# A static order of all steps of an attention and token-mixing kernel is replaced by another

## The chip, the cores and the metric

The kernel runs on one core of one Trainium2 chip. It is measured in device microseconds: three runs of the kernel as it was gave a median of 230.96 us (230.74 to 232.75).

## The reference

There are two parts, of 8 batches with 576 positions each. The first is attention with 8 heads of 64: one coarse attention on q, k and v averaged over groups of 4 positions, its result repeated 4 times, plus one local attention in which a position sees the positions less than 4 away.

```python
out_d = sm_attn(q_d, k_d, v_d)                 # 144 coarse positions
out_up = np.repeat(out_d, factor, axis=2)      # factor = 4
mask = np.abs(pos[:, None] - pos[None, :]) < factor
scores = np.where(mask, scale * np.matmul(q, k.transpose(0, 1, 3, 2)), -1e9)
...
return (out_up + out_local).astype(np.float32)
```

The second takes the result x, of 512 channels, through a rotation and two mixings.

```python
theta = x @ w_theta
zr, zi = x * np.cos(theta), x * np.sin(theta)
y = np.einsum('ts,bsd->btd', w_tok_r, zr) + np.einsum('ts,bsd->btd', w_tok_i, zi)
u = x + y
return (u + np.maximum(u @ w_ch, 0.0)).astype(np.float32)
```

## The kernel before, in words

All work is written as small steps, each with a two-letter name, a tuple of numbers (the batch first) and a place. The string ORDER lists the steps; a loop walks through it and issues each one. A chain of dependencies without semaphores (the function `pin`) keeps the instructions of each engine in the order in which they were issued. So ORDER sets the order on every engine, and with it which engine waits for whom. The letter behind a step is its engine (v VectorE, a ScalarE, g GpSimd); digits behind a TensorE step are its PSUM banks, of which there are 8; a digit or letter behind a load is its staging buffer, of which there are 14.

For one batch the steps are these. Loads are lk, lq (k and q, four each), lv and lw (two halves of a v tile, five each), all issued on SyncE's queue. Casts to bf16 are ck, cq and cv. TensorE transposes k and q in tp (for batch 7 a DMA does it, dk), and ev takes them out of PSUM into kT and qT. Means over 4 positions are kd and qd; pv and vd make those of v. The coarse attention is sd (scores), ed (exp), nd (numerator and denominator), xn (normalise), xd and xc (transpose into xdT). The local attention is ps (scores, three steps), ex (exp), mk (mask, a product with a 0/1 band), po (five steps), nm (normalise), xt (transpose) and xa (add both parts into xT). Steps ps, sd and po work on 64 rows of the array at a time.

The second part has th (x times w_theta), cs (cosine and sine on ScalarE), xm (x transposed back) and zz (the products z). The last 64 positions of a batch go another way: tt, ct, zt, zp, zc (dz, a DMA, for the later batches). Token mixing is mx, eight steps of nine matmuls, and ua adds x. Then come ch (u times w_ch), up and uc (u transposed; du, a DMA, for the later batches), rl (relu and add) and st (store). The last 64 positions of two batches are joined in ut, dt, ht, rt, ss and sr. Weights are loaded, cast and, for the token weights, transposed on TensorE in wp and taken out in wc, all before the first mx. The v of batch 0 takes a path of its own, by contiguous rows: loads l1, casts c1, transposes t1, evictions e1 (into xT of the other parity), then x1, which gathers the overlapping windows on TensorE, and cv.

Steps wm issue idle matmuls on a zero tile. Steps te and ts load ScalarE's tables for Exp and Sin ahead of their use. Buffers rotate by fixed rules: kT, z, uT and most others by the parity of the batch, pm through 4, tmp through 6, the denominators rl through 2.

In ORDER, a step's numbers are not written: each kind of step takes its next set of numbers, so that all steps of a kind run in one fixed sequence, by batch and then by number.

Of the kernel before, what the change touches and what calls it, by code (L numbers as in the profile page):

```python
# [57 lines left out]
l10 l11 c1g c1g k0 l12 lk3 l14 ckg c1v lk5 wm0b t101 c1g e1a kcg wm24 t123 e1a lq6 wm45 x12 cva ckg x13 cva x10 cvv  # L58
cqg lq7 lk8 lk9 tp45 cqg kcg kcg x12 lqa eva lqb kdg cvv kca cka wm62 tp67 lkc x13 lkd cvv eva ckv wm13 pv01 cqv lq0
la2 cqg lb1 tp45 qdv eva wm22 tp23 eva wm65 ps67 kdg vdv lq3 qdv ckg cka ps45 cag ex wm25 sd23 ex lb4 ed cbg lk5 sd01  # L60
cqg ps67 mkv ed po45 nm po23 nd45 nd01 la6 nm la7 xn xn lk8 mkg tp23 cag po45 ex xt6 po01 cqa eva la9 lqa mkg caa xd7
lqb ckg xca ckg nm tp23 nm xt4 xt5 lbd cag lbc cbg lb2 xt7 xa cqg lb1 eva lb0 cbg lb3 lb6 tp01 xa po23 th4 xa xm5 xa
lv7 cqg nm cbg th6 lw xt7 cbg th2 lv5 xm3 evv cbg ts cs tp01 lv8 lv9 cs cbg xa tt4 zz cs xm5 wp6 wp2 zz lw lw wp3 lw
lv4 lw cbg lqa zz ct lqd eva qdg ztv wp7 cba th4 wcv zp5 lkb xm6 wcv lkc kdg wcv wp2 wp3 wcv zcv wp0 wcv wp1 cs wp7
wca wcv ps45 lk2 lk1 wcv wcv ps23 te ex qdg ps01 lq0 zz kdv cva ex mx7 mx6 mx4 cvg ua sd23 cvg cvg mkv lc3 ex po01 ua
sd67 ed ed mkv mx5 ua nm po23 ua po01 cvg pv67 nm nm mkg vda mx4 ua po23 lq6 cqg po67 nd01 nm nd45 mx2 up3 xn lq7 ckg
xn cqg lk5 cka nm tp01 xd4 lk8 up5 uca eva xcv xt3 ucv lk9 tp67 cka xt4 xt0 ua ckg xt1 kdg lv4 xa xa xa mx5 xa eva lva
tp23 ua th4 xt0 lw xa evv cqg th5 xm1 lvb lcd lqc tt0 lw lk1 lv2 lv0 lw ts cs lw xm4 cqg cs tp67 ckg cqg th2 xm3 th5
ct lw cka zz tp01 cs qdg zz cs xm2 evv ztg lc6 lc5 zp4 mx6 ccg zz qdg zcv zz eva cvg mx7 ps45 te ex ua ps23 ua ckg kdv
ex mkv ps01 mx6 lq7 mx7 po45 sd23 ex lq8 lk3 kdg ed cvg sd01 cqg ckg ua lk4 lq9 mx6 tp23 mkv lva lw lvc lw nm ua tp45  # L70
up7 cvg mkv cvv ed mx0 eva cvg pv23 ccg ua ucv eva po67 po45 ua nm up1 nm vda ccg ccg ch0 nd67 lq1 xn nd23 lkb cqg cqa
tp45 uca qdg xn mx1 xd2 xt3 eva ps67 rl lq0 ua po45 xcv kdg qdg ps01 ch2 xa ckg ex mkg nm rl mx3 ps67 cqg lv2 cka po45
ex ua sd01 lkd xt2 ckg ex nm mx3 xt4 xt5 xa up2 ua cqa cqg tp67 cvv ed up3 xa evv uca th0 xa lv6 xt1 up2 xa lw th4 xm6
ucv ts cs uca th5 cvg lq5 ckg po01 cvg zz cs nm po23 xm7 cs ch6 nm tt4 tp01 lw ct tp23 th5 rl mkg ch4 lq7 zz st eva
evv rl po67 sd01 cs cqg cvg ztg po23 ch5 nm nm rl ch4 lv8 lw te ed cvg st pv67 vda zp0 zca lk4 cka lk3 lk1 tp23 cqa
mkg ckg lq9 lqb rl qdg lva lw xm1 eva ckg utg lv0 zz lw xm5 ch4 nd67 lvc zz xn lw nd01 mx5 lvd xn mx6 st ps23 rl lv2
ua po01 kdg nm ps45 ua mx7 lk5 ex xd0 cqa xt1 ex up6 ua xcv ucv lk6 kdv tp23 cqg utg mx0 tp45 qdg xa ua eva sd67 xt2
lv8 xt3 ch1 eva xa mkg ed xa th0 mkv rl cvg lk3 lw xt6 xt7 xa xa lw lk1 cvg th2 mx1 ua ts cs xm3 cvg tt0 zz th6 st lq4
cs cvg cka po45 dt cvg ckg ct po23 th7 mx1 ztg lk7 cs lvb nm pv45 cs ckg po67 cqg kdg lw nm ua sd23 mx0 cvg nm te ed
zp1 tp67 vdv zcv ht2 tp45 xm1 rt lw ua lq9 mx3 eva zz ps67 eva ua lva qdg po45 nm ex ps01 lq0 ex xm2 up3 zz lqc nd67  # L80
uca lvd tp45 cqa xm2 qdg xn nd01 zz mx3 cka cka xn mx2 xd0 up1 lk2 lv6 kdg st ua mx3 cqa mkv lw uca xcv eva tp67 xt0
up1 lk5 ua ua cva ucv xt4 xa mx5 st xa st eva ps23 mkg sd01 qdg po67 lw ed ua nm lv3 xt4 mx5 xt6 cva mx7 po01 ua ex
sd23 xa xa po45 lw nm cvg th6 nm lq4 cqv xt0 lw ed cvv xa ts cs tp23 mkv lv8 th1 cs xm4 ua ch5 kdg lw rl ch6 lv9 eva
tt0 th1 th7 xm5 pv23 utv ct ztg zz up0 ss cqg cs zz vdv mx1 uca ua xm0 lv1 lw st zz cs tp45 lv7 cvg lv0 cvg lqb nd23
xm7 ch1 eva kdg rl nd45 xn mx0 rl xn dz ch1 sr ps23 ps45 lw lw qdg lw te ex lka zz po67 ua mx0 ex ps23 cqa ex nm rl ua
lkd ps67 mkv po45 mx1 up0 mkg nm ckg sd23 po45 ua mkg lqc nm ex sd67 utg cka cvg lv6 uca mx1 ch0 cva xt4 ua st st xd1
xca cvg mx5 ed mx1 ed up2 lw xa ua rl xt3 ua uca pv45 cqg po67 xa lq4 nm po01 xt2 cvv th3 up6 vda ucv lq3 xt7 mx4 ch5
ckg st dk8 cqa xt6 nm xa rl st dkb th2 xa cqg nd01 ch5 ckg xm7 xa xn evg ht6 ts cs eva dt tt3 zz du nd01 lv5 rl du cs
ct xm5 qdv th7 cva xn zz cs mkg th2 cs dk2 ztg ua lv1 eva dk9 mx3 dz ua st xm7 kdg rt zz evg ch5 xm4 up2 uca qdg sr zz
xd3 lw mx6 xcv mx4 xt7 po01 ps23 te ex ua rl ua mx6 kdg nm po45 utv du xa ua po01 ps23 xt7 xa mx6 ex xt7 th2 nm ua xa  # L90
ts cs mkg lw ch3 du lv7 mx6 st nm sd45 rl cvg ps01 ua ss po23 nm te ex xt7 mx6 xt2 mx3 xa ed xa po01 lw du mkg ua st
# [666 lines left out]
```

## Time and profile before

| What | Value |
|---|---|
| median of 3 runs | 230.96 us (230.74 to 232.75) |
| span of the profiled execution | 229.4 us |
| mean granted TensorE clock | 0.996 |
| TensorE matmul busy | 219.7 us (96%) |
| VectorE busy | 185.6 us (81%) |
| ScalarE busy | 159.3 us (69%) |
| GpSimd busy | 144.1 us (63%) |
| TensorE on the chain that ended last | 86% of the span |
| moved by DMA | 49.35 MB, mean 215 GB/s |

The profile is of one execution, which is not one of the three runs; its own time is its span plus what lies around it, and the median of the runs is 1.56 us above the span. Matmuls are pipelined, so a busy TensorE is not one at its peak. A line such as L610 is a line of the kernel before. PE is TensorE, PEld its weight loads, DVE VectorE, ACT ScalarE, POOL GpSimd, SP SyncE and SPq its queue of DMA issues.

### The profile page before, as it was taken

The page shows a single profiled execution, that of the slowest core. Times are in us where ns is not written, and L with a number is a line of the kernel's source. Part 1 is how long each engine was busy: PE and PEld are TensorE (multiplying, and loading weights), DVE is VectorE, ACT ScalarE, POOL GpSimd, SP SyncE. Part 2 cuts the span into 40 slices and gives each one's busy share as a digit, 9 for nine tenths or more (in the row PEclk, how much of TensorE's full clock was granted, in tenths as well). Part 3 has the DMA queues.
Part 4 walks back from the last instruction along what each step waited for, and adds up shares of the span by engine and source line. Part 5 has one row for each costly group of instructions (what it writes and reads, how often), then busy time and mean ns, then how long its engine had stood idle before and what let it go on. Part 6 is the DMA issues. An engine that isn't in the chain of part 4 may idle for free.

```text
span 229.4 us, 8506 instructions
## 1 busy us (share of the span) xinstructions
PE 219.7 (96%) x3491; PEld 154.2 (67%) x3491; DVE 185.6 (81%) x377; ACT 159.3 (69%) x239; POOL 144.1 (63%) x190
## 2 busy tenths in 40 slices
PE   7898899999999999999999999899999999999992
PEld 2455778696778765776788667676676665677740
DVE  5168999999899899797898969979898889476382
ACT  2389899759987899689887896779879258600000
POOL 7768999929999989991984456892697310200000
PEclk9999999999999999999999999999999999999998
DMA  6999999999989999999998007996576357376677
GB/s 181 387 391 391 268 190 222 374 271 226 235 270 249 248 345 177 231 261 233 291 220 211 21 17 191 302 214 126 136 132 187 68 118 206 74 207 160 94 239 241
DMA packets 76647, 49.35 MB, mean 215 GB/s; under 512 B 61120, under 2 KB 61120, under 8 KB 76608
## 3 DMA queue, kind: packets, MB, share of 16 engines
q1 hardware_dynamic: 76608, 48.81, 83.4%
q8 instruction: 27, 0.44, 0.8%
q14 instruction: 12, 0.10, 0.1%
HBM read 33.98 MB, written 9.44 MB: 189 GB/s over the span
## 4 chain that ended last, share of the span: by engine, by line
PE 86%; DVE 7%; DMA 3%; issue 2%; SPq 1%; ACT 0%; POOL 0%; DVEq 0%
PE PS L610 30%; PE PS L548 12%; PE PS L635 12%; PE PS L304 5%; PE PS L531 4%; PE PS L512 3%; DMA st<-in_v_dram 3%; PE PS L587 2%; PE PS L483 2%; PE PS L448 2%; PE PS L560 2%; DVE tmp L521 2%; PE PS L624 2%; PE PS L652 2%; PE PS L453 1%
## 5 line engine op out<-in xcount | busy, mean ns | idle before, releaser
L610 PE MATMUL PS<-WT,z 128*128 128x288 bf16 x576 | 77.9, 286 | 0.2 <-issue 0.2
L610 PEld LDWEIGHTS <-z 128*128 128x128 bf16 x576 | 54.3, 98 | 15.8 <-issue 0.9
L615 DVE TENSOR_TENSOR uT<-PS,xT 128x288 bf16<-128x288 f32 x64 | 28.8, 452 | 11.8 <-PE PS L610 10.9
L548 PE MATMUL PS<-wth,xT 128*128 128x512 bf16 x128 | 32.2, 379 | 0.0
L635 PE MATMUL PS<-wch,uT 128*128 128x512 bf16 x128 | 31.1, 379 | 0.0
L569 POOL TENSOR_TENSOR zT<-xT,cst 128x512 bf16<-128x512 bf16 x7 | 8.1, 1153 | 34.0 <-ACT cst L566 34.0
L521 DVE TENSOR_TENSOR tmp<-PS,rl 128x512 bf16<-128x512 f32 x40 | 27.7, 692 | 1.4
L502 POOL TENSOR_TENSOR pm<-pm,band 128x1024 bf16<-128x1024 bf16 (+1 forms) x14 | 25.0, 1789 | 4.5 <-ACT pm L491 4.5
L537 DVE TENSOR_TENSOR xT<-PS,xdT 128x464 bf16<-128x464 f32 (+1 forms) x40 | 24.0, 629 | 3.0 <-ACT xdT L471 2.0
L640 DVE SCALAR_TENSOR_TENSOR osb<-PS,ur 128x512 f32<-128x512 f32 x32 | 21.8, 685 | 4.7 <-PE PS L635 4.2
L491 ACT ACTIVATE pm<-PS 128x1024 bf16<-128x1024 f32 (+1 forms) x24 | 20.4, 879 | 6.5 <-PE PS L483 6.5
L553 ACT ACTIVATE cs<-PS,pihc 128x512 bf16<-128x512 f32 x32 | 22.2, 693 | 1.6 <-PE PS L548 1.4
L720 ACT ACT_TABLE_LOAD x15 | 19.2, 1283 | 0.3
L331 POOL TENSOR_TENSOR two<-kT 128x580 f32<-128x580 bf16 x13 | 15.0, 1152 | 7.0 <-ACT kT L317 5.3
L635 PEld LDWEIGHTS <-uT 128*128 128x128 bf16 x128 | 11.9, 98 | 11.1
L554 ACT ACTIVATE cs<-PS 128x512 bf16<-128x512 f32 x32 | 19.2, 601 | 0.0
L594 DVE TENSOR_TENSOR z<-PS,cs 128x1024 bf16<-128x1024 bf16 x24 | 16.0, 682 | 2.3 <-PE PS L587 1.8
L548 PEld LDWEIGHTS <-xT 128*128 128x128 bf16 x128 | 11.3, 98 | 9.6 <-DVE xT L537 0.2
L331 POOL TENSOR_TENSOR two<-qT 128x576 f32<-128x576 bf16 x13 | 14.9, 1145 | 4.3 <-ACT qT L317 4.0
L438 ACT ACTIVATE pd<-PS 128x864 bf16<-128x864 f32 x16 | 13.8, 888 | 5.0 <-PE PS L427 4.9
L397 POOL CAST v_w<-st 128x512 bf16<-128x512 f32 x26 | 16.8, 672 | 0.0
L317 ACT COPY qT<-PS 128x1152 bf16<-128x1152 bf16 x13 | 14.6, 1121 | 2.0 <-PE PS L304 2.0
(116 smaller groups left out, 427.0 us busy)
## 6 DMA issues: line engine op xcount, KB each, us to landing
st<-in_k_dram SPq DMA_DIRECT2D x32, 288.0 KB, 6.0
st<-in_q_dram SPq DMA_DIRECT2D x32, 288.0 KB, 6.1
st<-in_v_dram SPq DMA_DIRECT2D x70, 128.0 KB, 5.2
out_dram<-osb SPq DMA_DIRECT2D x32, 256.0 KB, 2.4
st<-in_v_dram SPq DMA_DIRECT2D x4, 288.0 KB, 3.2
st<-in_moe_w_tok_r_dram SPq DMA_DIRECT2D x4, 288.0 KB, 6.5
st<-in_moe_w_tok_i_dram SPq DMA_DIRECT2D x4, 288.0 KB, 7.4
st<-in_moe_w_theta_dram SPq DMA_DIRECT2D x4, 256.0 KB, 6.3
```

What stands on the lines that cost most here:

```text
L331: nc.gpsimd.tensor_tensor(out=t, in0=src[:, :, 0:2], in1=src[:, :, 2:4], op=ALU.add)
L491: nc.scalar.activation(out=pm[(3 * b + u) % NPM][:, :, 0:n].rearrange("p e c j w -> p e (c j w)"), in_=at.pop(("ps", b, u))[:, :, 0:4 * W ...
L502: EW[w].tensor_tensor(out=t, in0=t, in1=m, op=ALU.mult)
L521: nc.vector.tensor_tensor(out=tmp[(NCH * b + c) % NTMP].rearrange("p g (j d) -> p g j d", d=D), in0=ps[:, :, :, 0:D], in1=r.unsqueeze(3).t ...
L537: nc.vector.tensor_tensor(out=xT[b % 2][:, :, CH * c:CH * c + cnt].rearrange("p e (m j) -> p e m j", j=4), in0=at.pop(("xt", b, c))[:, :, ...
L548: nc.tensor.matmul(out=ps, lhsT=xT[b % 2][:, dc, P * c:P * c + P], rhs=wth[:, dc, :], start=(dc == 0), stop=(dc == 3))
L553: nc.scalar.activation(out=t[:, 0, :], in_=ps, func=AF.Sin, bias=pihc, scale=1.0)
L554: nc.scalar.activation(out=t[:, 1, :], in_=ps, func=AF.Sin, bias=0.0, scale=1.0)
L610: nc.tensor.matmul(out=ps, lhsT=z[b % 2][:, j, P * dc:P * dc + P], rhs=WT[:, j, cols], start=(j == 0), stop=(j == 8))
L615: nc.vector.tensor_tensor(out=uT[b % 2][:, dc, cols], in0=at.pop(("mx", b, i)), in1=xT[b % 2][:, dc, cols], op=ALU.add)
L635: nc.tensor.matmul(out=ps, lhsT=uT[b % 2][:, dc, P * c:P * c + P], rhs=wch[:, dc, :], start=(dc == 0), stop=(dc == 3))
L640: nc.vector.scalar_tensor_tensor(out=o, in0=at.pop(("ch", b, c)), scalar=0.0, in1=ur[b % 2][:, c, :], op0=ALU.max, op1=ALU.add)
```

## The change

ORDER is another list. It holds the same steps, with new engines for some of them, new banks and staging buffers, and it writes out the numbers of every step (`tp010.01` is tp with batch 0, half 1, operand 0, in banks 0 and 1), so that steps of a kind can stand in any sequence: ps 2 ahead of ps 0, mx 5 ahead of mx 2. The list follows a planned time over all engines, with loads taken to land later than in the plan of the old list, and with idle matmuls placed where TensorE is half idle. There are 20 idle matmuls (37 before), all ahead of the first sd and behind it none, 13 table loads (15 before), and five buffers rl instead of two. Among the steps that may go to several engines VectorE gets two more ev, two more qd, three more zt, one more ck, cq, uc and xc, and one less kd, mk, vd and zc and three less wc.

```diff
 ORDER = """
-l10 l11 c1g c1g k0 l12 lk3 l14 ckg c1v lk5 wm0b t101 c1g e1a kcg wm24 t123 e1a lq6 wm45 x12 cva ckg x13 cva x10 cvv
-sd67 ed ed mkv mx5 ua nm po23 ua po01 cvg pv67 nm nm mkg vda mx4 ua po23 lq6 cqg po67 nd01 nm nd45 mx2 up3 xn lq7 ckg
...
+lk02.0 lk03.1 kc3.a l100.2 lq01.3 l101.4 lq00.5 l103.6 ck02.a l102.7 lk01.8 ck03.v lk00.9 kc0.g lq03.a c100.v kc2.g
+nd11.23 xn11.v ck20.g po10.01 lq33.d tp211.45 nm10.v ev211.a po11.67 lv23.1 nm11.v mx07.2 ua07.v xd1.3 lw21 xc1.v
...
-    rl = tiles(2, [P, 2, 4], "rl", FP32)
+    rl = tiles(NCH, [P, 2, 4], "rl", FP32)
...
-        r = rl[c % 2]
+        r = rl[c]
...
-    todo = {kind: iter(seq) for kind, (_, seq) in STEPS.items()}
+    todo = {(kind,) + tuple(args) for kind, (_, seq) in STEPS.items() for args in seq}
     for word in ORDER.split():
-        kind, place = word[:2], word[2:]
+        word, _, place = word.partition(".")
+        kind, args = word[:2], tuple(int(x) for x in word[2:])
...
-        STEPS[kind][0](*next(todo[kind]), place)
+        todo.remove((kind,) + args)
+        STEPS[kind][0](*args, place)
         pin()
```

Two places show what moves. The first is the start of SyncE's queue of loads, here as it was (st0 to st11 are the staging buffers, each takes one tile of two heads).

```order
L367 DMA st0_127<-in_v_dram 128x576
L367 DMA st1_128<-in_v_dram 128x576
L367 DMA st2_129<-in_v_dram 128x576
L288 DMA st3_130<-in_k_dram 128x576
L367 DMA st4_131<-in_v_dram 128x576
L288 DMA st5_132<-in_k_dram 128x576
L288 DMA st6_133<-in_q_dram 128x576
L288 DMA st7_134<-in_q_dram 128x576
L288 DMA st8_135<-in_k_dram 128x576
L288 DMA st9_136<-in_k_dram 128x576
L288 DMA st10_137<-in_q_dram 128x576
L288 DMA st11_138<-in_q_dram 128x576
```

And the same twelve places of SyncE's queue now (L399 loads v, L320 k and q).

```order
L320 DMA st0_130<-in_k_dram 128x576
L320 DMA st1_131<-in_k_dram 128x576
L399 DMA st2_132<-in_v_dram 128x576
L320 DMA st3_133<-in_q_dram 128x576
L399 DMA st4_134<-in_v_dram 128x576
L320 DMA st5_135<-in_q_dram 128x576
L399 DMA st6_136<-in_v_dram 128x576
L399 DMA st7_137<-in_v_dram 128x576
L320 DMA st8_138<-in_k_dram 128x576
L320 DMA st9_139<-in_k_dram 128x576
L320 DMA st10_140<-in_q_dram 128x576
L320 DMA st11_141<-in_q_dram 128x576
```

Both are the twelve tiles of batch 0. The loads of v have moved from the front to the middle, and two of k have come to the front.

The second place is VectorE behind its constants, up to the first mask product (pm). As it was (v_w0 is v by windows, k_tm and q_tm are k and q in bf16, qd0 the means of q, vd0 those of v):

```order
L395 CAST v_w0_70<-PS_61 128x8x64 x3
L297 CAST k_tm1_75<-st9_136 128x8x64
L297 CAST k_tm1_75<-st9_136 128x64
L297 CAST q_tm1_78<-st10_137 128x8x64
L297 CAST q_tm1_78<-st10_137 128x64
L323 TENSOR_REDUCE qd0_68<-qT0_64 128x288
L413 CAST vd0_72<-PS_61 128x8x64
L416 CAST vd0_72<-PS_61 32x4x64 x2
L323 TENSOR_REDUCE qd0_68<-qT0_64 128x288
L502 TENSOR_TENSOR pm0_83<-pm0_83,band_145 128x1024
```

And the stretch of VectorE now that begins with the cast of the tenth load and reaches the first mask product.

```order
L329 CAST k_tm0_74<-st9_139 128x8x64
L329 CAST k_tm0_74<-st9_139 128x64
L329 CAST q_tm1_78<-st10_140 128x8x64
L329 CAST q_tm1_78<-st10_140 128x64
L329 CAST q_tm1_78<-st11_141 128x8x64
L329 CAST q_tm1_78<-st11_141 128x64
L427 CAST v_w0_70<-PS_61 128x8x64
L355 TENSOR_REDUCE qd0_68<-qT0_64 128x288
L427 CAST v_w0_70<-PS_61 128x8x64
L355 TENSOR_REDUCE qd0_68<-qT0_64 128x288
L427 CAST v_w0_70<-PS_61 128x8x64
L534 TENSOR_TENSOR pm0_83<-pm0_83,band_148 128x1024
```

The casts of k and q now stand ahead of the evictions into v_w0, of which there are still three and which now alternate with the means; vd0 has gone to ScalarE. Ahead of this stretch VectorE casts one tile each of k, v and q and takes out one transposed q.

More of the change, by code (lines that the diff above doesn't have):

```diff
@@ L98 @@
+rl72.v st71 st72 ch70.2 rl70.v st70 ht3.0 rt3.v sr3 ch73.1 rl73.v st73 ss3
 """
@@ L722 @@
             continue
-        STEPS[kind][0](*next(todo[kind]), place)
+        todo.remove((kind,) + args)
+        STEPS[kind][0](*args, place)
         pin()
-    for kind in todo:
-        assert next(todo[kind], None) is None, kind
+    assert not todo, todo
     assert set(x[0] for x in at) <= {"v", "ot"}, at
```

109 lines of the change are left out of this document (70 added, 39 removed).

## The prediction

> **What bounds the kernel now.** I read the span and the shares of the engines first, then the engines by stretches, then the chain that ended last, then the waits.
>
> ```profile
> core 0: 229.4 us, clock 0.996
> ...
> PE 219.7 (96%) x3491; PEld 154.2 (67%) x3491; DVE 185.6 (81%) x377; ACT 159.3 (69%) x239; POOL 144.1 (63%) x190
> ...
> 0.00:30.00 30.00, 26.00 (x411) 15.85 (x412) 20.24 (x54) 19.91 (x26) 24.56 (x52) 1.00 0.97 323
> 30.00:90.00 60.00, 59.76 (x1146) 44.66 (x1144) 55.84 (x108) 52.32 (x82) 53.53 (x68) 1.00 1.02 255
> 90.00:140.00 50.00, 50.00 (x840) 36.97 (x839) 42.62 (x87) 42.28 (x63) 33.81 (x42) 1.00 0.79 184
> 140.00:150.00 10.00, 9.06 (x224) 6.49 (x223) 8.52 (x17) 5.86 (x10) 7.32 (x8) 1.00 1.04 285
> 150.00:220.00 70.00, 70.00 (x859) 48.14 (x857) 53.77 (x108) 38.90 (x61) 24.87 (x24) 1.00 0.66 140
> ```
>
> The stretches give the stretch, its length, then busy time of PE, PEld, DVE, ACT and POOL with instruction counts, the granted clock, the DMA share and GB/s. From 30 to 220 us PE is busy for 59.76 + 50.00 + 9.06 + 70.00 = 188.82 of 190 us, at full clock. So 1.2 us of idle time is all that a better order can take out of these 190 us without removing PE work, and the change removes none of it there: the same transposes and matmuls run. What is not PE-bound is the head, up to the first token-mixing matmul (mx, L610), and the tail.
>
> ```profile
> 2.67 5.95 DMA st<-in_v_dram
> ...
> 9.39 0.69 PE PS L378 x9
> ...
> 14.59 0.69 DVE v_w L395
> 15.28 0.91 DVE k_tm L297 x2
> 16.19 0.94 DVE q_tm L297 x2
> 17.13 1.26 DVE qd L323
> 18.39 0.60 DVE vd L413
> ...
> 19.78 1.35 DVE qd L323
> ...
> 22.83 0.52 issue
> ...
> 28.83 0.99 PE PS L548 x4
> ...
> 38.36 3.41 PE PS L610 x27
> ```
>
> This is the chain of work in order of time (start, length, what). In the head it runs through v of batch 0 (its landing, then its transpose on PE) to the eviction into v_w on VectorE, where the last casts of k and q (15.28, 16.19) stand behind the v_w evictions although they have nothing to do with them. VectorE then carries most of the chain until the normalised tiles are transposed. The first channel matmul (th, L548) starts at 28.83, mx at 38.36.
>
> **The change part by part.**
>
> The first 12 loads (SP). They are the same 12 tiles, of one size, in another order.
>
> ```profile
> 4.73 1.74 SPq L288 DMA_DIRECT2D st<-in_k_dram  x2
> 6.51 1.72 SPq L288 DMA_DIRECT2D st<-in_q_dram  x2
> ...
> st<-in_k_dram SPq DMA_DIRECT2D x32, 288.0 KB, 6.0
> ```
>
> The 10th load is issued near 6.4 and the 12th near 8.2 (near the ends of these rows); with 6.0 us to landing (the median of such a load) they are there by about 12.4 and 14.2, whichever tiles they are. In the new order the 10th is k 0,0 and the last two are q. VectorE now casts k 0,0 (ck00), q 0,3 and q 0,2 one behind another. At 0.93 us each (rows 0.91 and 0.94), from 12.4, the third ends at 15.2; in the row above it ends at 17.13. VectorE is 1.9 us ahead there.
>
> VectorE up to the first mx. Behind that point the new order gives VectorE more before the last input of mx (zc0): three v_w evictions, one mask multiply, the copy xc0 and the mean qd10; and less: vd0, zt0 and three copies of WT.
>
> ```profile
> L502 DVE TENSOR_TENSOR pm<-pm,band 128x1024 bf16<-128x1024 bf16 x7 | 5.7, 814 | 0.0
> ...
> L323 DVE TENSOR_REDUCE qd<-qT 128x288 bf16<-128x1152 bf16 x3 | 4.0, 1346 | 0.0
> ...
> L279 DVE COPY WT<-PS 128x576 bf16<-128x576 bf16 x8 | 3.1, 442 | 0.0
> ...
> L471 DVE COPY xdT<-PS 128x576 bf16<-128x576 bf16 x5 | 2.2, 447 | 0.0
> ...
> L395 DVE CAST v_w<-PS 128x512 bf16<-128x512 f32 x3 | 2.1, 692 | 6.3 <-PE PS L390 6.3
> ...
> L569 DVE TENSOR_TENSOR zT<-xT,cst 128x512 bf16<-128x512 bf16 x1 | 0.7, 724 | 0.0
> ```
>
> Added: 3 x 0.69 + 0.81 + 0.45 + 1.35 = 4.7. Removed: vd0 (18.39 to 19.78 in the chain, 1.4) + 0.72 + 3 x 0.44 = 3.4. So 1.3 us of the 1.9 is given back, and I take **-0.6** for the head. All five normalisations and both batch means (nm, xn) now stand ahead of the first xa, so th begins no earlier than before, with more of the small PE steps already done. Bounds: -2.4 if none is given back and the half microsecond of "issue" at 22.83 goes too; above nothing, +1.7, worked out at the clock rival below.
>
> Idle matmuls. The order has 20 where it had 37, all in the head.
>
> ```profile
> L715 PE MATMUL PS<-warm 128*128 128x512 bf16 x37 | 10.2, 407 | 0.0
> ...
> L227 PE MATMUL PS<-warm 128*128 128x512 bf16 x6 | 2.7, 630 | 1.3 <-DVE warm L198 1.3
> ```
>
> They fill time in which PE waits, so taking 17 away is worth nothing; what it costs if their cover is gone is the clock. The first six took 630 ns each as a mean, 2.7/6 = 0.45 us of PE apiece, the later ones 10.2/37 = 0.28: PE starts at a lower speed. The granted clock reads 1.00 as a mean of every stretch above, so after those first six nothing was slow. In the new order only three idle matmuls follow the first six before the first k transposes, whose casts cannot be ready before about 6.3 (the second load's landing, then 0.9 of cast on VectorE behind its constants), and PE stands for about 1 us there; a slow start that lasts longer is a rival below. The Trainium skill ("TensorE: Matmul & The Clock Gate", Part 1) says that the array runs at half rate until it was busy through a free-running window of about 3.4 us, and falls back after an idle one. The slow first six agree with the first half of that; no run so far shows the fall.
>
> Switches of array shape. Steps ps, sd and po use 64-row tiles.
>
> ```profile
> 44.43 1.21 PE PS L610 x9
> ...
> 60.98 0.80 PE PS L483 x80
> ...
> 67.15 1.10 PE PS L610 x9
> ...
> 96.24 0.39 PE PS L483 x32
> ```
>
> An mx ahead of a po (44.43) occupies PE 1.21 us, one ahead of a transpose (67.15) 1.10, so going in costs 0.11. Three ps in a row (two of 32 matmuls, one of 16: two and a half units) take 0.80, one of 32 alone 0.39; so 1.5 units are 0.41, a unit 0.27, and coming out costs 0.12. Counted in the two orders from the first mx on, there were 22 ways in and 26 out (the others pass through pv, whose 6 ways in cost the same), and now 28 and 31 (with 5): 10 more, since lone steps stand between po steps (po10 tp211 po11, where po11 and po12 stood together). 10 x 0.11 = **+1.1**, on PE itself, with nothing to hide it.
>
> Waits that go and come.
>
> ```profile
> DVE uT L615 <- PE PS L610: 10.9, 21, 0.9
> ...
> PE PS L512 <- DVE tmp L521: 0.9, 1, 0.9
> ```
>
> Behind the head, PE's longest wait is that of po for a PSUM bank that nm must empty, once, 0.9 us. With another order this place does not exist in its old form; I count all of the 1.2 us as gone: **-1.2**. New ones of this kind come, since banks are as few as before (8) and the new order evicts each almost as soon as it is full, so that the next user follows closely. The trace cannot show them. Below: nothing. Above: the 3.4 us of the VectorE rival. I take **+1.0**, near to what the old order has, since it shares out the same banks in the same way.
>
> Off the path: one Exp table and one Sin table less on ACT (two loads, and ACT is at 42.28 of 50 us or under from 90 on); rl in five buffers instead of two, which only lets the normalisations run in any order; loads issued earlier against their casts, where PE waits for no landing behind the head.
>
> The tail.
>
> ```profile
> 202.80 14.33 PE PS L610 x117
> 217.14 6.91 PE PS L635 x32
> 224.04 0.88 PE PS L652 x4
> ```
>
> It was 13 mx, eight ch and ht3, with one VectorE step and two stores behind. Now it is again a run of mx and eight ch, with ht3 ahead of the last ch, one VectorE step and two stores: **0**. du73, the transposing DMA for the last results, has four ch (4 x 0.86) to cover it.
>
> Sum: 229.4 - 0.6 + 1.1 - 1.2 + 1.0 = 229.7 us of span. The median of the runs, 230.96, is 1.6 above this span, which lies around it. So **231.3 us**.
>
> **The rivals.**
>
> VectorE becomes the bound (slower). Between 30 and 90 us it is busy for 55.84 of 60, idle 4.2. Counted in the order from the first mx to the last step of batch 1, the new one gives it some 3.4 us more there: one more q or k eviction or mean (1.35), vd2 (1.4), two zt (2 x 0.72), one mask multiply less (0.81). 0.8 us stays idle. It decides once VectorE needs more waiting than that for its inputs; the 21 waits for mx in the row above, up to 0.9 each, say that it needs some. If it needs all 4.2, PE slips 3.4 in place of the 1.0: 229.7 + 2.4 + 1.6 = 233.7. Against: the VectorE steps that PE needs at once are few, and rl and ua of finished batches could lag. Place: th, po and mx waiting for xa, nm, zz or a bank of theirs between 45 and 95 us.
>
> Half clock in the head (slower). If full rate comes one window later, the nine idle matmuls ahead of the first v transposes last 9 x 0.45 = 4.1 in place of 9 x 0.28 = 2.5, and two transposes (0.69 at 9.39 in the chain) take twice as long, 1.2 more; less half a microsecond in which PE would wait for its casts anyway, some 2.3 us later for everything behind: the head is +1.7 in place of -0.6, and the time 233.6. For it: the head holds 17 idle matmuls fewer. Against: the granted clock stays at 1.00 with 4 us of gaps in the head now (PE 26.00 of 30).
>
> The head keeps its lead (faster). -2.4 in place of -0.6, and no new waits: 229.4 - 2.4 + 1.1 - 1.2 = 226.9, with 1.6 around it 228.5. For it: the casts of k and q no longer stand behind v. Against: the VectorE sum above.
>
> **How the numbers follow.** What counts as no change is within 1%, 228.65 to 233.27. The forecast, and what lies close to it, has 0.46; the head's lead 0.26; VectorE 0.19; the clock 0.09. The forecast's own range is 229.3 to 233.3, with new waits from nothing to 3 us. With the two slower rivals at 233.6 to 233.7, which may fall together with a wait of the forecast's kind, and the faster one with 1 us of doubt on its head, the range goes from 227.3 to 235.3. Faster than 1%: 0.26 (all of the head's lead). Slower: 0.28 (both of the others). Same: 0.46.
>
> **What would show it.** PE busy in the 10 us stretches from 40 to 220 within 0.3 of 10 each; the first mx between 36.5 and 38.5 in the chain; mx of 1.21 more often than before; VectorE busy for 58 or more of the 60 us from 30 to 90; a granted clock of 1.00 from the first stretch. I am wrong on the head if the first mx comes before 36 or after 39.5; wrong on the waits if PE loses over 3 us between 40 and 220; wrong on the clock if a stretch of the head shows less than 1.00 past 6 us.

## The result, and the profile after

The new order takes a median of 234.08 us (4 runs, 233.26 to 234.47) where the old one takes 230.96; the ratio is 1.0113, with a 95% interval from 1.0066 to 1.0160. Timed once more later, it took 235.32 us (6 runs, 233.43 to 236.09) beside 230.92 for the old order: 1.0176 (1.0136 to 1.0215). Ratios are of the means of the fast executions alone, while the medians are over all executions. The prediction was 231.3, within a range of 227.3 to 235.3, with "within 1%" as the likeliest case; the kernel came out slower, by 1 to 2 percent.

The profiled execution took 233.26 us, the fastest of the first four; its span is 231.6 us, so 1.7 us lie around it (1.6 was assumed). Its page says of the engines:

```profile
span 231.6 us, 8441 instructions
...
PE 219.9 (95%) x3474; PEld 154.5 (67%) x3474; DVE 185.6 (80%) x381; ACT 155.9 (67%) x242; POOL 139.2 (60%) x180
```

And by the same stretches as before, with the same columns (stretch, length, busy time of PE, PEld, DVE, ACT and POOL, granted clock, DMA share, GB/s):

```profile
0.00:30.00 30.00, 23.37 (x399) 15.09 (x400) 21.22 (x59) 21.11 (x28) 22.37 (x50) 1.00 0.95 333
30.00:90.00 60.00, 59.97 (x1126) 44.56 (x1125) 56.19 (x106) 53.23 (x85) 46.60 (x59) 1.00 0.89 263
90.00:140.00 50.00, 49.78 (x905) 36.31 (x902) 42.20 (x87) 41.37 (x63) 37.51 (x46) 1.00 0.75 193
140.00:150.00 10.00, 10.00 (x189) 7.15 (x188) 8.20 (x18) 8.49 (x16) 8.34 (x8) 1.00 0.58 148
150.00:220.00 70.00, 69.69 (x833) 48.30 (x831) 51.53 (x106) 31.72 (x54) 24.38 (x21) 1.00 0.69 140
```

PE is busy for 59.97 + 49.78 + 10.00 + 69.69 = 189.44 of the 190 us from 30 to 220. Before, it was 188.82. By this column PE stands still for less time than it did, and yet the span is 2.2 us longer. The column counts a matmul that waits a little, or takes a little longer because the array changes its shape, as busy.

So I took another measure: for each step of TensorE, the time from its start to the start of the next, less what a step of its kind takes when one of the same shape follows at once (1.10 us for mx, 0.86 for th and ch, 0.50 for tp, and so on; idle matmuls count for nothing). These shortest times sum to 196.80 us up to the last step, in both orders. What is left is lost:

| us | before | after | after, a second profile |
|---|---|---|---|
| lost up to the first mx | 19.05 | 19.55 | 20.17 |
| lost from there to the start of the last step | 8.03 | 9.76 | 11.51 |
| of that, switches of array shape | 5.25 (54) | 6.29 (64) | as many |
| of that, waits over 0.05 us | 1.81 (4) | 2.47 (19) | more, up to 1.2 each |
| from the start of the last step to the end | 5.52 | 5.45 | 5.46 |
| span | 229.4 | 231.6 | 233.9 |

Of the 2.2 us of the first profile, 0.5 lie in the head, 1.0 in switches and 0.7 in waits. The 0.5 is the difference of two single profiles and has scatter of its own: over the profiles that have one of the two heads unchanged, the first mx comes at 37.75 to 38.29 us in the old head (four) and at 38.55 to 39.38 in the new one (four), by the means 0.9 us later. The old order has four waits behind its first mx (1.13 us ahead of po54 at 146 us, 0.41, 0.16, 0.11); the new one has nineteen, the longest 0.37. The second profile (of the last run below; 235.65 us) is nearer to the median and has 2.3 us more of the head's and the waits' kind.

In the head of the new order, on PE (start, length, what; in brackets the idle time ahead of a group and what ended it):

```profile
3.79 1.49 PE L748 MATMUL PS<-warm 128*128 128x512 bf16 x3
6.90 1.14 PE L336 MATMUL PS<-ident,k_tm 128*128 128x128 bf16 x9 [1.62 <-ACT k_tm L329]
7.83 3.35 PE L748 MATMUL PS<-warm 128*128 128x512 bf16 x9
11.01 0.67 PE L410 MATMUL PS<-ident,z 128*128 128x128 bf16 x9
...
29.84 1.90 PE L580 MATMUL PS<-wth,xT 128*128 128x512 bf16 x8 [0.56 <-POOL uT L294]
...
38.80 1.40 PE L642 MATMUL PS<-WT,z 128*128 128x288 bf16 x10
```

Nine idle matmuls at 7.83 take 3.35 us, 0.37 each (the old order's later ones took 0.28), and the nine transposes at 6.90 take 1.14 where those at 11.01 take 0.67. TensorE runs at half speed here: where the clock came before these nine, in a run below, they took 2.11 us, 0.23 each. The trace's record of the granted clock begins, with 1.00, at 10.33 us (5.51 us in the profile of before); ahead of the first record the column of the stretches reads 1.00 too, so that it could not show this. The first th (L580) starts at 29.84, the first mx (L642) at 38.80.

On VectorE, in the same head:

```profile
13.93 0.96 DVE L329 CAST q_tm<-st 128x512 bf16<-128x512 f32 x4
15.51 0.69 DVE L427 CAST v_w<-PS 128x512 bf16<-128x512 f32 x1 [0.61 <-PE PS L422]
...
19.83 2.03 DVE L534 TENSOR_TENSOR pm<-pm,band 128x1024 bf16<-128x1024 bf16 x2
...
25.14 0.19 DVE L490 RECIPROCAL rd<-PS 72x8 f32<-72x8 f32 x1
...
28.60 2.28 DVE L569 TENSOR_TENSOR xT<-PS,xdT 128x464 bf16<-128x464 f32 x4 [0.51 <-PE PS L563]
```

In the old order the same first addition into xT stood at 27.55:

```profile
27.55 2.27 DVE L537 TENSOR_TENSOR xT<-PS,xdT 128x464 bf16<-128x464 f32 x4
```

The third cast ends at 13.93 + 0.96 = 14.89 (17.13 before), so VectorE was 2.2 us ahead. Then, but for two waits for PE (0.61 and 0.51), it works without a stop, and the first addition into xT comes 1.05 us later than before.

Last, two mx behind the first one, on PE. From its start to the start of the next step, an mx ahead of a step on 64 rows takes 1.21 us (64.45 to 65.66) and one ahead of a transpose 1.12 (66.04 to 67.16):

```profile
64.45 1.28 PE L642 MATMUL PS<-WT,z 128*128 128x288 bf16 x9
65.66 0.32 PE L515 MATMUL PS<-qT,kT 64*64 64x64 bf16 x16
...
66.04 1.28 PE L642 MATMUL PS<-WT,z 128*128 128x288 bf16 x9
67.16 0.67 PE L336 MATMUL PS<-ident,k_tm 128*128 128x128 bf16 x9
```

### The profile page after: what moved, and what is told of

It reads as the page before. It is cut to its first block, busy times and chain, and to the rows that moved or that the text cites. A ratio compares the mean times of both kernels' runs of the same rounds, so it can differ in the third digit from the quotient of the medians.

```text
span 231.6 us, 8441 instructions
## 1 busy us (share of the span) xinstructions
PE 219.9 (95%) x3474; PEld 154.5 (67%) x3474; DVE 185.6 (80%) x381; ACT 155.9 (67%) x242; POOL 139.2 (60%) x180
## 4 chain that ended last, share of the span: by engine, by line
PE 73%; DVE 4%; POOL 1%; issue 1%; DVEq 0%
PE PS L642 27%; PE PS L667 11%; PE PS L580 10%; PE PS L336 4%; PE PS L563 3%; PE PS L515 2%; PE PS L544 2%; PE PS L619 2%; PE PS L656 2%; PE PS L684 2%; PE PS L480 1%; PE PS L592 1%; PE PS L459 1%; PE PS L485 1%; DVE osb L672 1%; PE PS L437 1%
## 5 line engine op out<-in xcount | busy, mean ns | idle before, releaser
L642 PE MATMUL PS<-WT,z 128*128 128x288 bf16 x576 | 78.0, 286 | 0.0
L642 PEld LDWEIGHTS <-z 128*128 128x128 bf16 x576 | 54.2, 98 | 15.0 <-issue 0.3
L580 PE MATMUL PS<-wth,xT 128*128 128x512 bf16 x128 | 31.9, 379 | 0.6 <-POOL uT L294 0.6
L534 POOL TENSOR_TENSOR pm<-pm,band 128x1024 bf16<-128x1024 bf16 (+1 forms) x15 | 26.2, 1750 | 8.5 <-ACT pm L523 8.5
L363 POOL TENSOR_TENSOR two<-kT 128x580 f32<-128x580 bf16 x14 | 16.6, 1182 | 10.2 <-ACT kT L349 7.8
L580 PEld LDWEIGHTS <-xT 128*128 128x128 bf16 x128 | 11.6, 98 | 11.1 <-DVE xT L569 0.7
L349 ACT COPY kT<-PS 128x1152 bf16<-128x1152 bf16 x12 | 13.4, 1123 | 6.1 <-PE PS L336 4.5
L601 POOL TENSOR_TENSOR zT<-xT,cst 128x512 bf16<-128x512 bf16 x4 | 5.6, 1396 | 19.7 <-ACT cst L598 19.6
L662 POOL COPY ut<-uT 128x256 bf16<-128x256 bf16 x4 | 1.6, 397 | 26.1 <-DVE uT L647 26.1
L429 POOL CAST v_w<-st 128x512 bf16<-128x512 f32 x24 | 15.7, 678 | 0.0
```

The costliest lines, as they stand in the source:

```text
L534: EW[w].tensor_tensor(out=t, in0=t, in1=m, op=ALU.mult)
L580: nc.tensor.matmul(out=ps, lhsT=xT[b % 2][:, dc, P * c:P * c + P], rhs=wth[:, dc, :], start=(dc == 0), stop=(dc == 3))
L642: nc.tensor.matmul(out=ps, lhsT=z[b % 2][:, j, P * dc:P * dc + P], rhs=WT[:, j, cols], start=(j == 0), stop=(j == 8))
```

## The experiments

The theory going in was that the head costs 0.5 us, the switches 1.0 and small waits 0.7. The rivals were VectorE as the bound from 30 to 90 us, the late clock as the cause of it all, and the head alone.

**The clock released earlier** (new order, four more idle matmuls in the first group).

```diff
-wm.23 tp010.01 ev010.a
+wm.27 tp010.01 ev010.a
```

> The new order with seven idle matmuls in place of three in the first group behind the warm-up (L748), nothing else. They fill the gap from 5.3 to 6.9 us in which TensorE stood still in the new order, where the clock record says full speed from 10.33 us only (5.51 us in the old order). Theory (the late clock costs part of the head): full speed from about 7 us, the nine transposes of the first v at about 9.5 in place of 11.0 us, first mx 0.5 to 1 us earlier than 38.80, span 230.7 to 231.1 in place of 231.6. Rival (VectorE sets the head whatever TensorE's clock does): full speed earlier too, but first mx and span within 0.2 us of the new order's. Second rival (four more idle matmuls delay the first k transposes and all behind them): first mx later, span 232 or more.

Measured: 233.75 us, 1.0121 (1.0086 to 1.0157), span 231.8. Full speed from 4.72 us, and the first transposes of v at 9.37 in place of 11.01; but the first mx at 38.72 in place of 38.80. By its number the rival holds: 1.6 us gained on PE near 10 us are 0.1 us at the first mx. But one thing was new: the clock fell to half again from 21.8 to 25.2 us. VectorE's timeline here shows what became of the gain:

```profile
19.16 2.00 DVE L533 TENSOR_TENSOR pm<-pm,band 128x1024 bf16<-128x1024 bf16 x2
...
25.03 0.20 DVE L489 RECIPROCAL rd<-PS 72x8 f32<-72x8 f32 x1 [0.51 <-PE PS L484]
```

At its first mask product VectorE was 0.67 us ahead of the first profile (19.16 against 19.83). Then it waited 0.51 us for the coarse attention on PE (nd), which ran at half speed, and was 0.11 us ahead (25.03 against 25.14, where there was no such wait). So an earlier clock was worth 0.67 us, and the fall took most of it back. No run has the early clock without the fall; what the late clock costs the head by itself is not measured at the first mx.

**The clock alone, on the old order** (eight idle matmuls fewer in its first group).

```diff
-lk5 wm0b t101
+lk5 wm03 t101
```

> The old order with three idle matmuls in place of eleven in its first group, nothing else: the clock's part by itself, on the order that was faster. Theory: full speed later than the old order's 5.51 us (by one or two steps of 3.4 us), first mx 0.5 to 1.2 us later than 38.29, span 229.9 to 230.6. Rival (the clock in the first 10 us costs nothing, since TensorE waits for casts there anyway): full speed later, but first mx and span within 0.2 us of the old order's.

Measured: 231.67 us, 1.0015 (0.9993 to 1.0038), span 229.9, first mx at 38.56, 0.27 later. Full speed came at 4.95 us, no later than before, so the run doesn't show what it was made for. Eight idle matmuls fewer cost nothing that these runs can tell.

**One mask product out of VectorE's head.**

```diff
         todo.remove((kind,) + args)
+        if (kind,) + args == ("mk", 0, 0):
+            continue
```

> The new order without one of VectorE's mask products in the head (mk00, 1.0 us near 20 us), so that one local attention tile of batch 0 is not masked; nothing else changes. Theory (from 15.5 us on VectorE is busy without a stop and sets when xT of batch 0, th and the first mx come; TensorE and its clock do not): the first xa at 27.6 in place of 28.6, th and the first mx 0.8 to 1.0 us earlier, span 230.6 to 230.9. Rival (TensorE's late clock or the token weights set the first mx): first mx and span within 0.3 us of the new order's 38.80 and 231.6.

Measured: 233.35 us, 1.0098 (1.0067 to 1.0129), span 232.2. VectorE's and PE's timelines have

```profile
27.77 2.29 DVE L569 TENSOR_TENSOR xT<-PS,xdT 128x464 bf16<-128x464 f32 x4
```

```profile
29.02 1.90 PE L580 MATMUL PS<-wth,xT 128*128 128x512 bf16 x8 [0.15 <-DVE xT L569]
...
37.98 2.26 PE L642 MATMUL PS<-WT,z 128*128 128x288 bf16 x17
```

With 1.0 us of work taken off VectorE near 20 us, so that one tile stays unmasked, xT, th and the first mx come 0.83, 0.82 and 0.82 us earlier. This profile had the clock early (4.77 us) and the fall at 21.8 us, as three others of the new order's variants had with both masks; their first mx came at 38.55, 38.72 and 38.80, 0.57 to 0.82 later than here. So VectorE's work sets the head, with PE's clock behind some of its waits. The span didn't follow (232.2 where 230.6 to 230.9 was expected): behind the first mx this profile holds 3.88 us of waits where the first one of the new order held 2.47 and the second one about 4.2.

**The two orders put together at the first mx**: the new head with the old order behind it, and the other way round.

```diff
 (all of the new order up to the first mx)
-mx01.0 cv10.g lk32.5 ex11.a mk12.v ...
+(the old order from its first mx on, without what is done already)
```

> The new order up to the first mx, the old order behind it (where the two leave steps of batch 1 in different states, the missing ones are moved to the nearest place), so 54 switches of array shape behind the first mx in place of 64. Theory (of the 2.2 us of span lost, 0.5 lies ahead of the first mx, 1.0 in switches and 0.7 in small waits behind it): first mx near 38.8, time lost by TensorE behind it back to 8.0 us, span 229.9, that is 0.5 over the old order and 1.7 below the new one. Rival (the head costs it all, through the lead that VectorE, ScalarE and GpSimd have or lack when the steady part begins): waits of TensorE behind the first mx stay, span 231 to 231.6. Rival (the order behind the first mx is not to blame, but VectorE's load between 30 and 90 us): VectorE has the old load here, so also near 229.9; told apart by the run with VectorE relieved.

> The old order up to the first mx with its 37 idle matmuls, the new order behind it, with its 64 switches of array shape. Theory: first mx near 38.3, TensorE loses 9.5 to 9.8 us behind it as in the new order, span 231.1, that is 1.7 over the old order and 0.5 below the new one. Rival (it is the head that costs the time): span 229.4 to 229.9.

Measured: 238.45 us, 1.0329 (1.0295 to 1.0364), span 237.5, and 238.31, 1.0305 (1.0269 to 1.0341), span 236.1. Both miss, by 5 to 8 us, and for a reason of their own: at the seam the first mx is to go into a bank that the ps just ahead of it have filled and exp (L517) has yet to empty. The new head's row at the seam, on PE:

```profile
43.22 5.88 PE L636 MATMUL PS<-WT,z 128*128 128x288 bf16 x27 [4.17 <-ACT pm L517]
```

Three mx take 5.88 us in place of 3.3: PE waited for 4.17 us, and the clock fell with it (rows below). By start-to-start times PE lost 6.9 us from there to the fourth step behind it, and 5.2 in the other run; without these the spans would be 230.6 and 230.9, where 229.9 and 231.1 were expected. That is an argument, and no measurement of the two halves. What the runs do show is that the number of switches goes with the order behind the seam, and their price with the number: 54 at 5.27 us and 64 at 6.29.

**Work taken off VectorE** (new order; three steps to GpSimd, one to ScalarE).

```diff
-zt1.v  zt2.v  kd20.v  vd2.v
+zt1.g  zt2.g  kd20.g  vd2.a
```

> The new order with four steps taken off VectorE between 45 and 90 us: zt of batches 1 and 2 and one kd of batch 2 go to GpSimd, vd of batch 2 to ScalarE (some 4 us of VectorE's 56 in these 60 us). Theory (VectorE does not bound these stretches; TensorE was busy for 59.97 of 60 us there): time within 0.5 us of the new order's 234.08, span 231.4 to 232. Rival of the prediction (VectorE is the bound between 30 and 90 us): span lower by up to 2.4 us, 229.2 to 230.5.

Measured: 237.20 us, 1.0270 (1.0233 to 1.0308), span 234.7. Neither: it is 3 us slower. PE's waits and GpSimd's work there:

```profile
57.52 1.18 PE L335 MATMUL PS<-ident,q_tm 128*128 128x128 bf16 x18 [1.22 <-DVE z L625]
...
60.48 0.40 PE L610 MATMUL PS<-ident,zT 128*128 128x128 bf16 x4 [0.92 <-POOL zT L600]
```

```profile
53.74 1.15 POOL L362 TENSOR_TENSOR two<-kT 128x580 f32<-128x580 bf16 x1
54.97 0.67 POOL L365 TENSOR_TENSOR kd<-two 128x290 bf16<-128x290 f32 x1
55.58 1.88 POOL L328 CAST q_tm<-st 128x576 bf16<-128x576 f32 x3
...
59.28 1.15 POOL L600 TENSOR_TENSOR zT<-xT,cst 128x512 bf16<-128x512 bf16 x1
```

The mean that GpSimd now makes (1.15 + 0.67 us) stands ahead of its casts of q, and PE waits 1.22 us for the last of these (its release is put down to VectorE, which had long been done); zT comes late too. So the run can't judge VectorE: it shows that GpSimd has no more room there than VectorE has.

**Switches taken out of the new order.**

```diff
-po10.01 lq33.d tp211.45        -sd21.67 ... mx12.1
+tp211.45 po10.01 lq33.d        +mx12.1 ... sd21.67
 (and po22 right behind po21, mx27 ahead of po44)
```

> The new order with four steps of TensorE moved by a place or two so that steps on 64 rows stand together: tp211 ahead of po10, po22 right behind po21, mx27 ahead of po44, mx12 ahead of sd21. Switches of array shape behind the first mx: 56 in place of 64. Theory (a switch costs 0.105 us on TensorE and nothing hides it): 8 x 0.105 = 0.85 us less, span 230.75 in place of 231.6, time 232.4 to 233.3 where the new order has 234.08, as far as no new wait takes some of it back. Rival (VectorE or another engine sets the pace, and TensorE only fills): the switches go, waits of the same size come, span 231.4 to 231.8.

Measured: 236.53 us, 1.0239 (1.0204 to 1.0274), span 234.0. The switches went as expected, 56 at 5.47 us (0.82 less). In their place came 3.6 us of waits. One of them stands where mx12 had stood between sd21 and ps22: PE now waits 1.1 us ahead of po20.

```profile
65.49 0.29 PE L514 MATMUL PS<-qT,kT 64*64 64x64 bf16 x16
66.74 0.32 PE L543 MATMUL PS<-v_w,pm 64*64 64x65 bf16 x16 [0.96 <-ACT pd L469]
```

The lone mx was what PE did here while exp was under way: it cost two switches and covered a longer wait. For the other three moves no such place is shown, and part of the 3.6 us can be scatter, since the second profile of the unchanged new order has 1.7 us more of waits than the first.

**The price of a switch by itself** (old order, twelve single idle matmuls: once between steps on the whole array, once between steps on 64 rows).

```diff
-mx10.7 ps20.45 te ex20 ua07 ps21.23
+wm.51 mx10.7 ps20.45 te ex20 ua07 ps21.23        (and eleven like it)
```

```diff
-mx10.7 ps20.45 te ex20 ua07 ps21.23
+mx10.7 ps20.45 te ex20 ua07 wm.31 ps21.23        (and eleven like it)
```

> The old order with twelve single idle matmuls (128 rows, 0.213 us of TensorE each) added behind the first mx, each between two steps that use the whole array, so that no switch of array shape is added (54 as before). It gives the base for the run beside it. Theory (TensorE bounds the time there, and what it is given comes on top): 12 x 0.213 = 2.6 us more than the old order, span 231.6 to 232.0. Rival (TensorE's work is hidden behind another engine): less than 1.3 us more.

> The same twelve idle matmuls in the same twelve neighbourhoods, but each between two steps on 64 rows, so that each adds a way out and a way in: 78 switches behind the first mx. Theory (a switch costs TensorE 0.10 to 0.12 us, with nothing to hide it): 24 x 0.105 = 2.5 us more than the run beside it, span 234.1 to 234.6. Rival (a switch costs nothing of its own, and what looks like it in the traces is waiting that would be lost otherwise): within 0.6 us of the run beside it.

Measured: 233.17 us, 1.0103 (1.0079 to 1.0126), and 235.24, 1.0193 (1.0169 to 1.0217), on one chip; spans 230.9 and 233.6. One of the places on PE, first without the idle matmul between the steps, then with it (the record of the idle matmul itself is missing there):

```profile
60.58 0.87 PE L509 MATMUL PS<-qT,kT 64*64 64x64 bf16 x80
61.38 2.01 PE L636 MATMUL PS<-WT,z 128*128 128x288 bf16 x15
```

```profile
60.44 0.46 PE L509 MATMUL PS<-qT,kT 64*64 64x64 bf16 x32
61.15 0.58 PE L509 MATMUL PS<-qT,kT 64*64 64x64 bf16 x48 [0.25 <-issue]
61.66 1.77 PE L636 MATMUL PS<-WT,z 128*128 128x288 bf16 x13
```

From ps to mx it is 0.80 us, and with the matmul between them 1.22: 0.21 for the matmul and 0.21 for two switches. The 24 switches cost 2.7 us by the spans, 0.11 each, and 2.07 by the medians, 0.09 each. The theory holds against its rival (within 0.6 us): where PE is as full as here, a switch is time of TensorE. The run beside it missed its own range. By the spans it is 1.5 us over the old order's profile, by the medians 2.25, where 2.6 was expected; its first mx came at 37.75, 0.5 us earlier, and from there to the last step it took 2.0 us more. So some 0.5 us of the added matmuls went into time that PE loses anyway. With the lower base the second span, 233.6, lies under its range too.

**The clock held through the head** (new order, six more idle matmuls between 19.7 and 21.6 us).

```diff
-mk00.v po04.67 la0.a sd00.45 ed00.a mk01.v po00.01
+mk00.v wm.43 po04.67 la0.a sd00.45 ed00.a mk01.v wm.03 po00.01
```

> The new order with six idle matmuls more, three ahead of po04 and three ahead of po00 (19.7 to 21.6 us), where the new order has none and the old one had twelve. In the profiles of four of its variants the granted clock fell to half for one window of 3.41 us near 22 us, behind a window in which TensorE was busy for 48 to 53 percent; of the four runs of the new order two have a mean clock of 0.991 to 0.993. Theory (this fall costs up to 0.6 us and is what lifts the median of the new order, 234.08, above its profiled run, 233.26): no half window behind 6 to 10 us, mean clock of every run at 0.995 or more, median 233.0 to 233.5. Rival (VectorE has the work of 20 to 28 us anyway and the fall is hidden): clock mended, median 233.9 to 234.3. Second rival (the added matmuls delay po and pv): median above 234.5.

Measured: 233.84 us, 1.0109 (1.0070 to 1.0147), span 232.1. Four of five runs have a mean clock of 0.998 or more, one 0.993; the median lies between what the theory and its first rival say, 0.24 below the first median of the new order and well inside its scatter. Stretches of 3.4 us (columns as above), first of this run, then of the new order's first profile and of its second, then of the new head with the old order:

```profile
20.40:23.80 3.40, 3.11 (x93) 1.84 (x92) 3.30 (x8) 2.60 (x5) 3.40 (x5) 1.00 1.05 368
23.80:27.20 3.40, 3.18 (x74) 2.92 (x72) 3.26 (x9) 3.35 (x5) 2.49 (x5) 1.00 1.01 304
```

```profile
20.60:24.00 3.40, 1.98 (x81) 1.64 (x81) 3.30 (x8) 2.76 (x6) 3.40 (x5) 1.00 1.07 367
24.00:27.40 3.40, 3.25 (x75) 2.96 (x72) 3.26 (x9) 3.37 (x5) 2.57 (x6) 1.00 1.00 322
```

```profile
19.90:23.30 3.40, 1.56 (x74) 1.22 (x74) 3.33 (x7) 2.42 (x5) 2.79 (x4) 1.00 1.06 373
23.30:26.70 3.40, 3.40 (x40) 3.40 (x40) 2.76 (x8) 2.69 (x4) 2.96 (x5) 0.50 1.00 280
```

```profile
37.90:41.30 3.40, 1.15 (x84) 1.03 (x84) 2.13 (x3) 3.37 (x6) 3.24 (x6) 1.00 1.02 349
41.30:48.20 6.90, 4.98 (x21) 3.12 (x21) 1.99 (x4) 1.87 (x3) 4.66 (x7) 0.51 0.80 278
```

In the second profile PE is busy for 1.56 of 3.4 us and then runs at half speed for 3.4 us; in the first it is busy for 1.98 and keeps its clock. The added matmuls lift that to 3.11. In the head the fall costs about half a microsecond: in the second profile, as in the one with the clock released early, VectorE waits 0.50 us for the coarse nd on PE, and the first mx is 0.6 us later than in the first profile, which had no fall. In the whole time no such cost shows: of the ten executions of the new order, the three with a mean clock of 1.000 took 233.26, 234.12 and 236.09 us, the other seven 233.43 to 235.65, and the run that prevents the fall isn't measurably faster.

**The old order with seven steps moved**, in search of a version better than both.

```diff
-nm52 ... rl23        -ut4 ... ua51        -po54 ... sd61.67
+rl23 nm52            +ua51 ut4            +sd61 po54        (and four more)
```

> The old order with seven steps moved by a few places on their own engines, where a replay of its trace (measured durations and waits, no other source) lets TensorE wait less: nm52 behind rl23, ut4 behind ua51, ua40 behind mk52 and ua17 behind cv30 on VectorE, ex30 behind ck41 on ScalarE, po54 behind sd61 and up11 behind th20 on TensorE. Theory (what is left to gain behind the first mx is the 1.8 us of waits, not the switches): 1.0 us less as an upper bound, span 228.4 to 229.2 in place of 229.4, time 0.1 to 1.0 below the old order's. Rival (the waits move on by one place, as they did when the new order was regrouped): span 229.4 to 230.

Measured: 231.25 us, 1.0003 (0.9984 to 1.0022), span 229.4. The rival holds. The run also has other banks for ps32, po24 and xt21. The wait of 1.13 us ahead of po54 is gone, and two others have grown: 1.25 us between xt21 and mx17 (where 0.41 was lost at that mx before) and 0.7 ahead of th51. No version that was tried beats the old order.

**The new order once more.**

> The new order once more, unchanged, for a median of more runs and a second profile. In its first profile the mask product on VectorE at 105.7 us took 0.68 us, while GpSimd waited for a load of k; in three of its variants it took 1.15 to 1.17 with GpSimd busy, and TensorE then waited up to 0.9 us for the bank that VectorE empties three steps later. Theory (the order leaves VectorE no slack there, and chance of the landings decides): median 233.8 to 234.4, 0.5 to 1.1 above the first profile's 233.26; the second profile shows either 0.68 and no wait there or about 1.15 and a wait. Rival (the first profile is typical): median 233.2 to 233.5.

Measured: 235.32 us, 1.0176 (1.0136 to 1.0215), above the theory's range and far above its rival's. The place near 105 us, on VectorE, in the first profile and in the second:

```profile
105.68 0.68 DVE L534 TENSOR_TENSOR pm<-pm,band 128x1024 bf16<-128x1024 bf16 x1
106.28 1.35 DVE L355 TENSOR_REDUCE kd<-kT 128x290 bf16<-128x1160 bf16 x1
107.55 1.34 DVE L349 COPY qT<-PS 128x1152 bf16<-128x1152 bf16 x1
108.82 0.67 DVE L672 SCALAR_TENSOR_TENSOR osb<-PS,ur 128x512 f32<-128x512 f32 x1
```

```profile
107.74 1.15 DVE L534 TENSOR_TENSOR pm<-pm,band 128x1024 bf16<-128x1024 bf16 x1
...
111.34 0.68 DVE L672 SCALAR_TENSOR_TENSOR osb<-PS,ur 128x512 f32<-128x512 f32 x1
```

And GpSimd at that time in the first, GpSimd in the second, and PE in the second:

```profile
106.36 0.67 POOL L329 CAST k_tm<-st 128x576 bf16<-128x576 f32 x1 [0.88 <-DMA st<-in_k_dram]
```

```profile
107.48 0.86 POOL L329 CAST q_tm<-st 128x576 bf16<-128x576 f32 x1
108.29 1.12 POOL L329 CAST k_tm<-st 128x576 bf16<-128x576 f32 x1
```

```profile
112.07 0.61 PE L619 MATMUL PS<-ident,xT 128*128 128x128 bf16 x8 [0.70 <-DVE osb L672]
```

Where GpSimd waits for a load of k, VectorE's mask product takes 0.68 us; where GpSimd has the tile and casts, 1.15, and GpSimd's casts are longer too. VectorE has the mean, an eviction and osb behind it without a gap, and PE waits for the bank that osb empties. The Trainium skill ("SBUF — State Buffer", "SBUF: two separate sides") says that a VectorE instruction with two SBUF inputs and a GpSimd instruction exclude each other at a shared pair of ports. The 0.68 and 1.15 agree. The product isn't always the one that is lengthened: at 41.65 us of the first profile it takes 0.68 beside a cast of v on GpSimd that takes 1.07 in place of 0.61. At this place the two profiles differ by whether a load of k had landed. It goes the other way too: the product at 125.0 us takes 1.20 in the first profile, and 0.68 in the second, at 127.5. The second profile also has a wait of 1.0 us at 75.7, within a step, which the trace puts down to "issue", that is to nothing that it shows; its cause stays open.

## Why the prediction was wrong where it was

Both medians, 234.08 and 235.32, lie above the forecast of 231.3 and above its own range, which ended at 233.3. The first lies within the stated range only because the two slower rivals had widened it to 235.3, and neither of them came about as it was priced; that the range held the result is luck.

**The head, -0.6: wrong; it was +0.5 in the first profile and +1.1 in the second.** VectorE's lead at the third cast was as forecast (2.2 us, 1.9 forecast), but by two errors that cancel: the three casts began at 13.49 and not at 12.4, behind the eviction of a q for which VectorE waits on PE, and took 1.4 us and not 2.8. The step that failed is "so 1.3 us of the 1.9 is given back". I summed VectorE's work up to the last input of mx. The place that decides is earlier, the first addition into xT, and by then 3.3 us were given back (2.2 ahead, 1.05 behind): the three evictions into v_w, a second mask product, a fifth normalisation (0.84) and xc0 now stand ahead of it, only vd0 has gone, and two waits for PE come on top (0.61 and 0.51, where there was one of 0.50). The 2.0 us that I took off for zt0 and the copies of WT lie behind that place and could not help th. I wrote that all five normalisations stand there and "so th begins no earlier than before", and gave it no price; th began 1.0 us later. The run without one mask product shows that it is VectorE that counts. Half of the delay came back by the first mx, where zt0 and the copies count too. The first mx at 38.80 and 39.38 missed the 36.5 to 38.5 that I named, and did not reach the 39.5 past which I called myself wrong: that line was too far off for an error of this size.

**Switches, +1.1: right.** 1.04 in the trace for ten more, and 0.09 to 0.11 each when measured by themselves. The rows that I read the way in from don't carry it, though: a piece of the chain reaches from one step's end to the next one's end, so that its length goes with the step ahead of it, and the mx at 67.15 stands ahead of pv and not of a transpose; from start to start it takes 1.20 us (66.99 to 68.19). The right size from these two rows was luck.

**Waits, -1.2 and +1.0: wrong in what was measured, and too small.** The idle time by stretches went from 1.18 to 0.56 us, so the -1.2 came about by half. But the column doesn't show waits of a few tenths. By start-to-start times they went from 1.81 to 2.47 us: +0.7 in the first profile where -0.2 was forecast, and about +2.4 in the second. "It shares out the same banks in the same way" was the wrong measure for them. The number of banks is the same, and the waits are not. My reading is that the new order has every engine close behind the one it feeds. Three places show it: a mask product 0.47 us longer (PE waits 0.70), a mean moved to GpSimd (PE waits 1.22), an mx moved by a few places (PE waits 0.96). For the other waits it is argued and not shown. The bound above, 3.4 us, held.

**The tail, 0, and 1.6 us around the span: right** (5.45 and 5.52 us; 1.7 us).

The terms for the first profile, with -0.6 replaced by +0.5 and -0.2 by +0.7, give 229.4 + 0.5 + 1.04 + 0.7 = 231.6, its span. The other 0.8 us of the first median, and 2.1 of the second, lie in executions that are longer than the one profiled first; the second profile shows for one of them that it is waits and the head, and for the rest it stays open.

**VectorE as the bound: not as I put it.** It was busy for 56.19 us from 30 to 90, not 58, and PE for 59.97. But a string of VectorE's steps without a gap does set PE at single places, near 106 us for one, which lies outside the place named.

**Half clock in the head: it came, and the price was wrong.** Full speed came at 10.33 and 9.68 us in the two profiles of the new order. I had 2.3 us for it; the run that releases the clock at 4.72 gained 0.67 at VectorE's first mask product and, with a fall behind it, 0.1 at the first mx. So the late clock can account for up to some 0.7 us of the head, about what the first profile lost there, and how much of the +0.5 is the clock and how much VectorE's own work stays open. The sign I named, a stretch with less than 1.00, couldn't show it in the first profile. The prediction said "no run so far shows the fall"; five of the profiles now do, in the head. All five have the new head (eight profiles do); none of the six with the old head does, which has twelve idle matmuls between 16 and 22 us. That these prevent it is argued; the run with six of them put back has no fall in its profile, but neither has the first profile without them.

**The head keeps its lead (0.26): no.** The chances leaned on the wrong side: I gave "slower" 0.28, all of it to the two rivals, and none to the forecast itself, although its own range reached 233.3 and its two unknown terms were bounded by +1.7 and 3.4. Both came out on the bad side. The first sign I named, PE busy for nearly all of each stretch from 40 us on, came true in a slower kernel: it was blind to what was lost.

## What to carry to other kernels

Where an engine is busy for 99 percent of its time, look at start-to-start times: waits of tenths and switches of shape don't show as idle time, and they were all of the 1.7 us lost behind the head. Price a reordering at the first instruction that the next stage waits for, not at the last. An order in which each engine follows close on another is worth less than its best execution says: profile it twice, and see what an instruction that takes half a microsecond longer does to it.

## What the runs showed of the hardware that was not expected

- The granted clock can fall behind a stretch in which PE works, but only about half of the time: 1.56 of 3.4 us busy, in several short gaps, then half speed for one stretch of 3.41 us. With 1.98 of 3.4 it stayed. It isn't a plain threshold on this column: in the run without a mask product 47 percent between 4.8 and 8.2 us was not followed by a fall, 48 percent between 18.4 and 21.8 was. The Trainium skill ("TensorE: Matmul & The Clock Gate", Part 1) gives idle gaps over about 3.4 us as the abstract rule, and for one kernel frequent short idle times between groups of matmuls as another way to lose the clock. The falls in the head agree with the second: PE did 74 matmuls in the stretch ahead of one, with no gap over 0.9 us. Gaps that add up to half of a stretch can be enough. At the seam of the joined orders the clock fell at 41.35 us, 2.3 us into a gap of 4.2.
- The grid of these stretches differs from run to run: over the profiles full speed came at 4.3 to 5.5 us in eight, 6.4 to 7.1 in two, and 9.7 to 10.6 in four. The late four all have an order with three idle matmuls in its first group, which in other executions was released at about 5.
- A mask product of 1024 columns on VectorE takes 0.68 us whenever GpSimd stands still (eight products in seven profiles), and 0.68 to 1.20 when GpSimd works.
- Casts of 512 columns that took 0.9 us with their small second part in the old head took 0.5 in the new one. Why isn't shown.
